# A PV pass between query projection and scores, and a new order of five key and value loads, in an attention and gated-FFN kernel

## The chip, the cores and the metric

The kernel runs on one core of one Trainium2 chip. The metric is device time in microseconds of one execution. A profile belongs to one execution, and its span is 1.8 to 2.1 us shorter than the time on the clock.

The engines are PE (TensorE, matmul), PEld (its weight loads, which overlap with matmuls), DVE (VectorE), ACT (ScalarE), POOL (GpSimd) and SP (which issues most transfers). "Head m" counts the 64 pairs of a block of 512 queries and one of 16 heads: four blocks, 16 heads each. "k6" and "v5" are the keys and values of the seventh and sixth of eight key/value heads; heads 10 and 11 read k5 and v5, heads 12 and 13 read k6 and v6.

## The reference, cut to what matters

```python
xn = layernorm(x)                                   # [1, 2048, 448]
q  = (xn @ wq) as 16 heads of 256
k, v = the last 512 rows of k_cache, v_cache, each of 8 heads used by 2 query heads
s  = softmax(q k^T / 16) v, heads joined, @ wo      # scores: 2048 x 512 a head
g  = silu((gelu(xn @ w_gate) * (xn @ w_up)) @ w_down)
return x + s * g
```

## The kernel before

Everything is recorded as operations with the buffers that they read and write; a small planner gives each a place on its engine and puts in the semaphore waits. FFN first, then attention. In attention PE alternates between a *query group* (the projection of 4, 6 or 8 heads by matmuls of 64 rows, two of which run side by side) and a run of scores and PV, 128 rows each.

```python
def q_group(n, pairs, more_act=False):        # two heads, four PSUM banks
    ...
    group(units, 0, QC, True, True)           # 64-row matmuls
    for i, b in enumerate(pairs):             # PSUM -> qT, half on ACT, half on DVE
        act(qT[:, s, 0, :], bank[b], ACT.Copy, (b_ps[b],), (b_qT[s][0],))
        ...
def s_mm(m):                                  # scores of one head: 4 tiles of 128 queries
    for t4 in range(4):
        b = AB[t4]
        mms([... qT x kT, 2 matmuls ...], [b_kT[g]] + b_qT[s], (b_ps[b],))
        ... ACT: p = exp(bank), row sums;  every second tile, DVE: 1/sum, pn = p * 1/sum
        dma_t(pT[...], pn[...])               # every second tile: transposed by a transfer

def pv(m):                                    # 8 matmuls: 2 halves e of 4 key blocks j
    for e in range(2):
        b = BB[m % 2 * 2 + e]
        mms([... va x pT ... for j in range(NJ)], [b_va[g]] + b_pT[x], (b_ps[b],))
        ... oTh <- bank on ACT or DVE
...
for m in range(NS):                           # NS = 64, LAG = 2
    if m in groups:                           # 0, 4, 12, 18, 26, 34, 42, 50, 58
        for i in range(m, hi, 2):
            p = (i - m) // 2
            q_group(i, ((cur, nxt[::-1], (cur[1], nxt[1])) if three else (cur, nxt) * 2)[p], end)
            ...
            if m == Q0 + QS and p == 0:       # m = 12
                K.reuse(...)
                for g in range(6, Hkv):
                    load_k(g)                 # transposing transfer
                for g in range(5, Hkv):
                    load_v(g)                 # plain transfer
                ...                           # Pool: 2 loads of g, 3 of x
    s_mm(m)
    ...
    if len(late) == LAG:
        pv(late.pop(0))                       # PV of head m-2
    ...
    late.append(m)
```

So PE's order in a run is: scores of m, PV of m-2, scores of m+1, PV of m-1, and so on. A PV has from its scores to its start two heads' time for exp, normalizing and the transposing transfer.

The softmax here doesn't subtract the row's maximum and nothing guards it: scores larger than these inputs give would overflow.

Of the kernel before, what the change touches and what calls it, by code (L numbers as in the profile page):

```python
# [168 lines left out]
def bass_recurrent_scan__sliding_block_cached__geglu_ffn__prompt_kernel(  # L169
# [13 lines left out]
    Hkv, Sk, Dh = A_k_cache.shape[1], A_k_cache.shape[2], A_k_cache.shape[3]  # L183
    HD = A_wq.shape[1]
    Hq = HD // Dh
# [6 lines left out]
    NJ = W // P  # L192
# [12 lines left out]
    Q0 = 4  # L205
# [6 lines left out]
    with es:  # L212
# [14 lines left out]
        def sbuf_bufs(at, size, n):  # L227
            return [K.buf(at + i * size, size) for i in range(n)]
# [35 lines left out]
        b_va = sbuf_bufs(a, NJ * Dh * 2, Hkv)  # L264
# [75 lines left out]
        b_pT = [sbuf_bufs(a + i * QC * NJ * 2, QC * NJ, 2) for i in range(NPT)]  # L340
# [25 lines left out]
        b_ps = [K.buf() for i in range(8)]  # L366
# [4 lines left out]
        groups = [0, Q0, Q0 + QS, Hq + 2] + list(range(Hq + 2 + QS, NQC * Hq, QS)) + [NQC * Hq]  # L371
# [181 lines left out]
        def bk(pairs, j):  # L553
            return pairs[j // 2] + j % 2
# [156 lines left out]
        def load_v(g):  # L711
            dma("sp", va[:, g, :, :],
                A_v_cache[0, g, Sk - W:Sk, :].rearrange("(j p) d -> p j d", p=P), (), (b_va[g],))
# [36 lines left out]
        cur, nxt = (0, 2), (4, 6)  # L750
        for n in range(4, NU, 2):
# [6 lines left out]
            cur, nxt = nxt, cur  # L758
# [24 lines left out]
            if n + 1 in DOWN_AT:  # L783
                def norms():
                    for f in (ln_a, ln_a, ln_b, ln_b):
                        f()
                end = down7(DOWN_AT[n + 1], (cur[0], cur[0] + 1, cur[1], cur[1] + 1, nxt[0], nxt[0] + 1),
                            (g2x[:, 0:2, :], g2x[:, 2:4, :]), b_g2x, then=norms if n < 28 else None)
                end(0, 1)
                end(2, 3)  # L790
                cur, nxt = (nxt[1], cur[1]), (cur[0], nxt[0])
# [10 lines left out]
        def q_group(n, pairs, more_act=False):  # L802

            c, h = divmod(n, Hq)
            units = [(b, lambda j, k, i=i: wq[:, k, (h + i) * Dh + j * P:(h + i) * Dh + (j + 1) * P],
                      wqr[:, h + i, :], slice(c * QC, (c + 1) * QC), b_wql[h // HG][:1], b_wql[h // HG][1:], b_xnT[c * 4:c * 4 + 4])
                     for i, b in enumerate(pairs)]
            group(units, 0, QC, True, True)
            for i, b in enumerate(pairs):
                s = qs(n + i)  # L810
                act(qT[:, s, 0, :], bank[b], ACT.Copy, (b_ps[b],), (b_qT[s][0],))
                if more_act and i:
                    act(qT[:, s, 1, :], bank[b + 1], ACT.Copy, (b_ps[b + 1],), (b_qT[s][1],))
                    continue
                K.op("dve", lambda v, s=s, b=b: v.tensor_copy(qT[:, s, 1, :], bank[b + 1]),  # L815
                     (b_ps[b + 1],), (b_qT[s][1],))

        AB, BB = [], []
        LAG = 2
        NS = NQC * Hq  # L820

        def s_mm(m):
            s, g = qs(m), m % Hq // 2
            for t4 in range(4):
                b = AB[t4]
                mms([(bank[b], qT[:, s, e, t4 * P:(t4 + 1) * P], kT[:, g, e, :], e == 0, e == 1) for e in range(2)],
                    [b_kT[g]] + b_qT[s], (b_ps[b],))
                n = m * 4 + t4
                r, z, y, x = n % NRS, n % NP32, n // 2 % NPN, n // 4 % NPT
                K.op("act", lambda e, b=b, r=r, z=z: e.activation(  # L830
                    p32[:, z, :], bank[b], ACT.Exp, scale=att_scale, accum_out=rsum[:, r:r + 1]),
                    (b_ps[b],), (b_p32[z], b_rsum[r]))
                if t4 % 2 == 1:
                    K.op("dve", lambda e, r=r: e.reciprocal(rden[:, r - 1:r + 1], rsum[:, r - 1:r + 1]),  # L834
                         b_rsum[r - 1:r + 1], b_rden[r - 1:r + 1])
                    for t in range(2):
                        K.op("dve", lambda e, r=r - 1 + t, z=(n - 1 + t) % NP32, y=y, t=t: e.tensor_scalar(  # L837
                            pn[:, y, t, :], p32[:, z, :], rden[:, r:r + 1], None, op0=ALU.mult),
                            (b_p32[(n - 1 + t) % NP32], b_rden[r - 1 + t]), (b_pn[y],))
                    dma_t(pT[:, x, t4 // 2, :, :, :].rearrange("p t j q -> p (t j) q"),  # L840
                          pn[:, y, :, :].rearrange("p t k -> p (t k)"), (b_pn[y],), (b_pT[x][t4 // 2],))

        def pv(m):
            h = m % Hq
            g, x = h // 2, m % NPT
            for e in range(2):
                b = BB[m % 2 * 2 + e]
                mms([(bank[b].rearrange("p (t q) -> p t q", q=P), va[:, g, j, e * P:(e + 1) * P],
                      pT[:, x, :, :, j, :].rearrange("p a t q -> p (a t) q"), j == 0, j == NJ - 1)
                     for j in range(NJ)], [b_va[g]] + b_pT[x], (b_ps[b],))  # L850
                i = 2 * h + e
                if e == 0 or m >= NS - LAG:
                    act(oTh[:, i, :], bank[b], ACT.Copy, (b_ps[b],), (b_oT[i],), scale=WS)
                else:
                    K.op("dve", lambda v, i=i, b=b: v.tensor_scalar(  # L855
                        oTh[:, i, :], bank[b], WS, None, op0=ALU.mult), (b_ps[b],), (b_oT[i],))
# [131 lines left out]
        late = []  # L988
# [6 lines left out]
        AB.extend(bk(cur, j) for j in range(4))  # L995
        BB.extend(bk(nxt, j) for j in range(4))
        for m in range(NS):
            if m in groups:
                hi = groups[groups.index(m) + 1]
                three = hi - m == 6  # L1000
                for i in range(m, hi, 2):
                    end = m > Hq and m % Hq == LAG
                    p = (i - m) // 2
                    q_group(i, ((cur, nxt[::-1], (cur[1], nxt[1])) if three else (cur, nxt) * 2)[p], end)
                    if m == 0:
                        sum_act(2, 2 + p)
                    if m == Q0 and p == 0:
                        K.reuse(b_kT[2:6] + b_va[3:5])
                        for g in range(2, 6):
                            load_k(g)  # L1010
                        for g in range(3, 5):
                            load_v(g)
                    if m == Q0 and p < 2:
                        gates3(2 * p)
                        gates3(2 * p + 1)
                    if m == Q0 + QS and p == 0:
                        K.reuse(b_kT[6:] + b_va[5:] + [b for y in b_xr for b in y])
                        for g in range(6, Hkv):
                            load_k(g)
                        for g in range(5, Hkv):  # L1020
                            load_v(g)
                        now = [[o for o in K.ops if o.eng == "pe"][-1]]
                        for t in range(NG2):
                            load_g2(t, now)
                        for t in range(NXR):
                            dma("pool", xr[:, t, :], x_view[:, t, :], (), b_xr[t], now)
                    if end and p:
                        burst_end((m // Hq - 1) * 4 + p - 1)
                    if m > Hq and m % Hq == LAG + QS and p == 1:
                        burst_end((m // Hq - 1) * 4 + 3)  # L1030
                if m == 0:
                    K.reuse([b for x in b_pT for b in x] + b_pn + b_p32)
            if m > Hq and m % Hq == LAG:
                K.reuse(b_pn + b_p32)
            s_mm(m)
            if m < LAG:
                if m == 0:
                    gates2 = down7(2, (BB[0], BB[1], AB[2], AB[3], BB[2], BB[3]), g2w, b_g2w, (3, 4, 6, 5, 2, 1),
                                   lambda: [sum_act(3, k) for k in range(4)])
                else:  # L1040
                    gates3 = down7(3, (BB[1], BB[0], AB[2], AB[3], BB[2], BB[3]), g2w, b_g2w, (3, 4, 2, 5, 6, 1),
                                   lambda: [gates2(q) for q in range(4)])
                    K.reuse(b_pT[2])
                if m == LAG - 1:
                    K.reuse(b_oT + [b for y in b_qT[:QS - Q0] for b in y])
                    assert not CASTS and not SUMS
            if len(late) == LAG:
                pv(late.pop(0))
            if m > Hq and m % Hq == LAG - 1:
                if m // Hq == 1:  # L1050
                    for b in [y for x in b_xs for y in x]:
                        b.old.extend(y for t in range(4) for z in b_xnT[t] for y in z.readers + [z.writer])
                burst(m // Hq - 1)
            late.append(m)
# [56 lines left out]
```

## Time and profile before

| | before |
|---|---|
| time, median of the first 3 runs | 540.66 us (540.63 to 542.68) |
| span of the profiled execution (a seventh run, 541.98 us on the clock) | 540.2 us |
| PE busy | 533.2 us, 99% |
| ACT, DVE busy | 58%, 71% |
| transfers of the instruction stream | 33 packets, 0.54 MB |
| pT transposes | 128, median 2.8 us from issue to landing |

The last two rows come from these lines of the page (queue and kind: packets, MB, share of 16 engines; and a transfer: count, median us to landing):

```profile
q8 instruction: 33, 0.54, 0.4%
...
pT<-pn SPq DMA_TRANSPOSE x128, 2.8
```

A note for reading PE: the profile gives each 512-column matmul a duration of 379 ns, while they follow each other every 216 ns. A gap of less than about 0.16 us is therefore no idle time in the profile. All gaps below are worked out from starts: start of the first matmul after the gap, minus start of the last before, minus 0.216. When a matmul's record is missing, its weight load, which is always recorded, stands for it.

### The profile page before, as it was taken

The numbers are of one execution on the slowest core, as the hardware profiler recorded it, in microseconds if no ns is written. First come the engines' busy times: TensorE is split into PE (matmuls) and PEld (weight loads), VectorE is DVE, ScalarE is ACT, GpSimd is POOL, SyncE is SP. The second block draws the span as 40 slices with busy tenths as digits, with TensorE's granted clock in tenths as the row PEclk, the third lists the DMA queues.
The fourth block names the chain that finished last, engine by engine and source line by source line (L and its number), as shares of the span: only waits on it lengthen the run. The fifth ranks groups of instructions, "written<-read, shape, count | busy, mean of one in ns | idle before, by whom it ended". The sixth has DMA issues, their size and how long they took to land.

```text
span 540.2 us, 10920 instructions
## 1 busy us (share of the span) xinstructions
PE 533.2 (99%) x4155; PEld 310.6 (58%) x4180; DVE 383.6 (71%) x839; ACT 314.2 (58%) x782; POOL 39.7 (7%) x78
## 2 busy tenths in 40 slices
PE   9999999999999999999999999999999999999998
PEld 5556656459644444984444469544444884444487
DVE  6689886798767757934875786367667934776785
ACT  5466355873568768116866850488488106876820
POOL 1131120000000010003001000120000003001010
PEclk9999999999999999999999999999999999999999
DMA  9569173932598686302861860067448302872821
GB/s 296 123 187 108 53 126 87 282 70 60 112 171 138 156 190 147 59 1 82 167 141 50 152 137 1 18 156 139 96 106 146 72 1 69 164 157 73 149 66 35
DMA packets 171604, 61.38 MB, mean 114 GB/s; under 512 B 155104, under 2 KB 168416, under 8 KB 171552
## 3 DMA queue, kind: packets, MB, share of 16 engines
q1 hardware_dynamic: 167488, 51.30, 45.0%
q0 software_dynamic: 3008, 8.72, 6.9%
q8 instruction: 33, 0.54, 0.4%
q10 hardware_dynamic: 1056, 0.66, 0.4%
q14 instruction: 19, 0.16, 0.1%
HBM read 19.76 MB, written 3.67 MB: 43 GB/s over the span
## 4 chain that ended last, share of the span: by engine, by line
PE 87%; ACT 4%; DMA 4%; DVE 3%; issue 1%; SPq 1%; ACTq 0%; DVEq 0%
PE bank L394 86%; ACT p L830 4%; DMA pT<-pn 2%; DVE pn L837 2%; DMA va<-in_A_v_cache_dram 1%; PE bank L511 1%; DVE rden L834 1%; SPq L382 1%; PE bank L492 0%; DVE oTh L855 0%; ACT oTh L385 0%; DVE xnT L884 0%; DVE gl L424 0%; DVE xnT L388 0%; DVE epst L425 0%
## 5 line engine op out<-in xcount | busy, mean ns | idle before, releaser
L830 ACT ACTIVATE p<-bank 128x512 f32<-128x512 f32 x256 | 150.6, 596 | 28.9 <-DVE pn L837 26.5
L394 PE MATMUL bank<-pT,va 128*128 128x512 bf16 x512 | 120.9, 379 | 0.8 <-DMA pT<-pn 0.5
L394 PE MATMUL bank<-kT,qT 128*128 128x512 bf16 x487 | 117.8, 379 | 2.3 <-ACT qT L385 1.0
L837 DVE TENSOR_SCALAR pn<-p,rden 128x512 bf16<-128x512 f32 x256 | 112.9, 483 | 8.7 <-DMA pT<-pn 4.4
L394 PE MATMUL bank<-xnT,wq 64*128 64x512 bf16 x768 | 94.9, 376 | 0.0
L394 PEld LDWEIGHTS bank<-pT,va 128*128 128x128 bf16 x512 | 49.4, 98 | 62.5 <-DMA pT<-pn 3.2
L394 PEld LDWEIGHTS bank<-kT,qT 128*128 128x128 bf16 x512 | 49.3, 98 | 61.7 <-issue 3.4
L394 PE MATMUL bank<-xnT,wgu 64*128 64x512 bf16 (+2 forms) x768 | 83.9, 350 | 0.1
L385 ACT ACTIVATE qT<-bank 128x512 bf16<-128x512 f32 x76 | 44.1, 596 | 51.6 <-PE bank L394 50.0
L815 DVE CAST qT<-bank 128x512 bf16<-128x512 f32 x52 | 34.8, 690 | 49.4 <-PE bank L394 49.4
L394 PEld LDWEIGHTS bank<-xnT,wq 64*128 64x128 bf16 x768 | 36.7, 94 | 46.3 <-ACT p L830 1.7
L394 PEld LDWEIGHTS bank<-xnT,wgu 64*128 64x128 bf16 x768 | 37.6, 94 | 36.0 <-issue 0.5
L834 DVE RECIPROCAL rden<-rsum 128x2 f32<-128x2 f32 x128 | 21.1, 165 | 48.3 <-ACT p L830 48.2
L830 ACT ACTIVATION_READ_ACCUMULATOR p<-bank 128x1 f32 x256 | 51.6, 202 | 0.0
L394 PE MATMUL bank<-wt,sr 128*128 128x224 f16 x512 | 50.0, 259 | 0.0
L394 PEld LDWEIGHTS bank<-wt,sr 128*128 128x128 f16 x512 | 49.0, 98 | 0.4 <-ACT oTh L385 0.2
L385 ACT ACTIVATE gl<-bank 128x512 bf16<-128x512 f32 x56 | 33.0, 596 | 26.4 <-PE bank L394 22.1
L560 DVE TENSOR_TENSOR actTh<-bank,gl 128x512 f16<-128x512 f32 x56 | 37.4, 688 | 11.3 <-PE bank L394 5.8
L855 DVE TENSOR_SCALAR oTh<-bank 128x512 f16<-128x512 f32 x62 | 42.3, 683 | 0.0
L385 ACT ACTIVATE oTh<-bank 128x512 f16<-128x512 f32 x66 | 38.9, 590 | 3.8 <-PE bank L394 3.8
L394 PE MATMUL bank<-wt,oTh 128*128 128x224 f16 (+1 forms) x416 | 38.4, 252 | 0.0
L394 PEld LDWEIGHTS bank<-wt,oTh 128*128 128x128 f16 x416 | 37.2, 98 | 0.9
(77 smaller groups left out, 387.8 us busy)
## 6 DMA issues: line engine op xcount, KB each, us to landing
wtb<-in_A_wo_dram POOLq DMA_DIRECT2D x4, 896.0 KB, 10.8
wq<-in_A_wq_dram SPq DMA_DIRECT2D x2, 1536.0 KB, 7.9
va<-in_A_v_cache_dram SPq DMA_DIRECT2D x8, 256.0 KB, 6.3
pT<-pn SPq DMA_TRANSPOSE x128, 2.8
xr<-in_A_x_dram POOLq DMA_DIRECT2D x15, 112.0 KB, 2.3
wd<-in_B_w_down_dram SPq DMA_DIRECT2D x1, 1568.0 KB, 7.5
g<-g_all POOLq DMA_DIRECT2D x14, 112.0 KB, 2.3
out_dram<-xr POOLq DMA_DIRECT2D x12, 112.0 KB, 2.1
```

What stands on the lines that cost most here:

```text
L382: K.op("sp", lambda e, o=o, i=i: e.dma_start_transpose(o, i), reads, writes, dma=True)
L385: K.op("act", lambda e, o=o, i=i: e.activation(o, i, func, scale=scale), reads, writes)
L394: ins = e.matmul(o, lhsT=l, rhs=r, start=st, stop=sp, skip_group_check=True)
L511: ins = e.matmul(bank[b][:, 0:w], lhsT=gl[:, 0, 0:P], rhs=gl[:, 0, 0:w], start=True, stop=True)
L560: K.op("dve", lambda e: e.tensor_tensor(actTh[:, c % 2, f, :], bank[b + 1], gl[:, s, :], ALU.mult), (b_ps[b + 1], b_gl[s]), (b_actT[c % 2] ...
L815: K.op("dve", lambda v, s=s, b=b: v.tensor_copy(qT[:, s, 1, :], bank[b + 1]), (b_ps[b + 1],), (b_qT[s][1],))
L830: K.op("act", lambda e, b=b, r=r, z=z: e.activation(p32[:, z, :], bank[b], ACT.Exp, scale=att_scale, accum_out=rsum[:, r:r + 1]), (b_ps[b] ...
L834: K.op("dve", lambda e, r=r: e.reciprocal(rden[:, r - 1:r + 1], rsum[:, r - 1:r + 1]), b_rsum[r - 1:r + 1], b_rden[r - 1:r + 1])
L837: K.op("dve", lambda e, r=r - 1 + t, z=(n - 1 + t) % NP32, y=y, t=t: e.tensor_scalar(pn[:, y, t, :], p32[:, z, :], rden[:, r:r + 1], None, ...
L855: K.op("dve", lambda v, i=i, b=b: v.tensor_scalar(oTh[:, i, :], bank[b], WS, None, op0=ALU.mult), (b_ps[b],), (b_oT[i],))
```

## The change

It aims at two kinds of waits. At six of the nine places where a query group ends and scores begin (heads 4, 18, 26, 34, 42 and 50), PE's list of waits names the copy of q out of PSUM; at the other three (0, 12 and 58) it shows a wait of the same kind with no cause, as "issue". At heads 12, 26, 34, 42, 50 and 58 one PV matmul, ready long before, now goes between. And at head 12 PV of head 10 waits for v5, which was issued behind k6 and k7; now v5 goes first. The banks of the last two query pairs are placed anew so that the PV matmul's bank is free early.

```diff
-        def pv(m):
+        def pv(m, part=None):
...
-                     for j in range(NJ)], [b_va[g]] + b_pT[x], (b_ps[b],))
+                     for j in range(NJ) if part is None or (part == 0) == (e == j == 0)], [b_va[g]] + b_pT[x], (b_ps[b],))
+                if part == 0:
+                    break
...
+            split = m in groups and m not in (0, Q0, Hq + LAG)
...
-   q_group(i, ((cur, nxt[::-1], (cur[1], nxt[1])) if three else (cur, nxt) * 2)[p], end)
+   q_group(i, ((cur, nxt[::-1], (cur[1], nxt[1])) if three else (cur, nxt, (cur[0], nxt[0]), (cur[1], nxt[1])) if split else (cur, nxt) * 2)[p], end)
...
+                        load_v(5)
                         for g in range(6, Hkv):
                             load_k(g)
-                        for g in range(5, Hkv):
                             load_v(g)
...
+            if split:
+                pv(late[0], 0)
             s_mm(m)
...
-                pv(late.pop(0))
+                pv(late.pop(0), 1 if split else None)
```

## The prediction

> **What bounds the kernel now.** I read the page's busy shares first, then the list of waits of PE, then the timeline of PE around the places that the change touches, then the chain of waits, and last the record of every transfer from issue to landing.
>
> The busy shares, the two largest matmul groups of the score stage (columns: busy us, mean ns of one, idle before) and PE's own list of waits:
>
> ```profile
> PE 533.2 (99%) x4155; PEld 310.6 (58%) x4180; DVE 383.6 (71%) x839; ACT 314.2 (58%) x782; POOL 39.7 (7%) x78
> ...
> L394 PE MATMUL bank<-pT,va 128*128 128x512 bf16 x512 | 120.9, 379 | 0.8 <-DMA pT<-pn 0.5
> L394 PE MATMUL bank<-kT,qT 128*128 128x512 bf16 x487 | 117.8, 379 | 2.3 <-ACT qT L385 1.0
> ```
>
> ```profile
> PE bank L394 <- ACT qT L385: 1.0, 6, 0.2
> ...
> PE bank L394 <- DMA pT<-pn: 0.5, 2, 0.3
> PE bank L394 <- DMA va<-in_A_v_cache_dram: 0.2, 1, 0.2
> ```
>
> PE is the bound from the first microsecond to the last: 533.2 of 540.2 us, at full granted clock. All that PE waits for by name is some 3 us. Two of these rows are what the change aims at: six waits of 0.2 us for the copy of q out of PSUM, at the six places where a query group gives way to scores, and one wait for v. So the whole prize, taken at face value, is 1.0 + 0.2 = 1.2 us of 540, or 0.2%.
>
> A busy share hides gaps, though, because a matmul's record lasts 379 ns while eight of them follow each other in 1.73 us, which is 0.216 us apart. So I worked from start times. The timeline of PE at head 26, the third of the six places, and the weight loads there, then the weight loads at the first down projection (49.9 us), where no query group is near:
>
> ```profile
> 289.72 1.46 PE L394 MATMUL bank<-xnT,wq 64*128 64x512 bf16 x12
> 291.33 1.67 PE L394 MATMUL bank<-kT,qT 128*128 128x512 bf16 x7 [0.16 <-ACT qT L385]
> 292.85 1.89 PE L394 MATMUL bank<-pT,va 128*128 128x512 bf16 x8
> ...
> 291.11 1.41 PEld L394 LDWEIGHTS bank<-kT,qT 128*128 128x128 bf16 x8 [0.42 <-issue]
> ```
>
> ```profile
> 49.91 0.50 PEld L394 LDWEIGHTS bank<-wdh,actTh 128*128 128x128 f16 x6 [0.42 <-issue]
> ```
>
> Two things are to be seen. Only seven of the eight score matmuls have a record, but all eight weight loads do, from 291.11 on: the first score matmul ran at about 291.12 and its record is missing. The "0.16 us wait" is mostly that hole. Second, the weight load before it came 0.305 us after the last 64-row matmul (290.800 to 291.105), and so did the one at 49.9 us (49.605 to 49.909), which goes from 64-row to 128-row matmuls as well and has nothing to do with q. The copy that the list names ended at 291.17, after the weight load had already begun, so it cannot have held it. The same distance (0.53 us with the hole) stands at all of the query-group ends, whatever ACT was doing. The real loss is the step from 64-row to 128-row tiles: 0.305 + 0.015 - 0.2 (normal distance of a pair to the next) = about 0.12 us each.
>
> The place where PE does wait is head 12, the third query group (chain of waits in that stretch, columns: start, us, what):
>
> ```profile
> 189.43 1.30 SPq L382
> 190.73 0.05 issue
> 190.78 1.29 SPq L382
> 192.07 0.04 issue
> 192.12 6.26 DMA va<-in_A_v_cache_dram
> 198.38 0.05 issue
> 198.42 1.68 PE bank L394 x7
> ```
>
> The two SPq entries are the issues of k6 and k7, 1.3 us each; v5 is issued only behind them, lands at 198.38, and PV of head 10 starts at 198.42. The last score matmul began at 197.86, and PV would have followed at 198.07. PE lost **0.35 us** there.
>
> **What the Trainium skill says.** "TensorEngine Tiling (Array Packing)", Key Properties: changing the tiling mode drains TensorE, changing the tile does not. The trace agrees, 0.12 us per change in either direction (0.10 from PV back to the query projection). "Perfetto Trace Analysis", Tensor Engine Instruction: the end of a matmul in a profile is computed, not observed. It agrees: 379 ns for what repeats every 216 ns, hence starts and not ends above. "DMA: Bandwidth & Descriptors", Queues, rings and completion order: transfers of one issuing engine are consumed in ring order, while different queues share the same 16 engines by turns. It agrees: k6, with nothing of Pool's beside it, took 3.19 us from issue to landing; k7, beside the g and xr loads that Pool issues from 190.66 on, took 5.34, and v5 behind it 6.26.
>
> **The change part by part.**
>
> *PV pass ahead of the scores (six places).* It moves one matmul of 0.216 us from behind the eight score matmuls to before them. The order listing shows the same 4180 matmuls and one semaphore instruction less on PE. PE's work is unchanged. The change from 64 to 128 rows stays, as PV has 128 rows too; only who pays it changes. Removed: about 0. The new waits: PV of head m-2 needs pT of that head (landed 9 to 35 us earlier), v, and its PSUM bank. To have this bank free, the last two query pairs are placed anew: its copy now stems from the third pair, which ended 3 us earlier. In exchange the third and fourth score tiles take banks that the fourth pair filled. At head 26 these copies end at 291.17 (ACT) and 291.26 (DVE), the third tile would need its bank at about 292.2: 0.9 us to spare. At heads 34, 50 the final sums of the burst stand before the copies on DVE, but the copy still ends at 352.65, when the tile needs it at 353.8. So no new wait here.
>
> *Scores 0.216 us later.* The exps of the first head start 0.65 us after its first weight load and would start 0.22 us later. Its transposed pT then lands 0.22 us later, for a PV that comes at the same time as before. I compared the landing of both halves of pT with the PV that reads them, head by head: first heads 12, 26, 42 and 58 have 1.58, 1.18, 1.19 and 1.18 us of slack. Heads 34 and 50 have 0.04, but there the first exp is held by an extra copy on ACT (it starts 1.09 us after, not 0.65), so it does not move. From the second head on, exps start when their tile is ready and the delay is made up. Cost: 0, at worst a few hundredths.
>
> *v5 first at head 12.* v5 would be issued at 189.43 in place of 192.12. When v3 followed a row of k loads at 156 us, it landed 1.8 us after the last of them; the transfer before v5 now lands at 190.88, so I estimate 192.7 for v5. It is needed earlier than before, at 196.34, since its PV pass now opens the scores. That leaves 3.6 us: the wait goes, **-0.35 us**. k6 is now second. It is needed at 196.34 + 0.22 = 196.56. In the kernel before, k7 in that position (beside Pool's five loads) landed 3.5 us after k6 (192.63 to 196.11). An estimate for k6: 192.7 + 3.5 = 196.2, 0.3 us before its need. v6, k7 and v7 are read from 203 us on and are safe.
>
> Sum: -0.35 (v5), 0 from the six passes, +0.1 as the mean of k6 being a little late: about -0.25 to -0.35, 540.66 - 0.3 = **540.4 us**.
>
> **Rivals.**
>
> *The waits for q are real.* Then six passes of 0.216 us each cover six waits of 0.16, together 1.0, and with v5 the time is 539.3. For it: the list of waits. Against: the missing record, the weight load that started before the named copy ended, and the same 0.42 us at 49.9 us.
>
> *k6 takes the place of v5.* With copies and transposes in turn and Pool's loads between, k6 could take as long as v5 did, 6.3 us from about 190.05, so 196.35, or as the slowest k (8.4 us), 198.4. The late case stops PE for up to 1.9 us with the PV pass already spent, and the time is 541 to 542. For it: every transfer from 190.7 to 193.3 took 4.6 to 7.5 us. Against: k6 stands second in its ring and most of that queue was behind it.
>
> *Shifted DMA coincidences.* Some pT transposes land 1 to 2 us late and stop PE (0.48 us at 174.97, 0.28 at 378.77, 0.34 at 419.05). In the packet records a 16 KB instruction packet precedes each of these by 3 to 4 us. They depend on phase; shifting the stream by 0.2 to 0.35 us can make one of them some tenths better or worse. This is worth plus or minus 0.3 us and has no preferred sign.
>
> **Range and chances.** The three runs before span 540.63 to 542.68, and two agree within 0.03. Gain fully kept: 540.3. Rival one would give 539.3, rival two 541 to 542; I give them one chance in ten and one in six. The 8-in-10 range is 539.6 to 541.2. 2% is 10.8 us, nine times all the PE waiting that the change could touch, so faster 0.005, within 2% 0.985, slower 0.01 (should k6 or v5 lag far beyond any transfer seen).
>
> **What would show it right or wrong.** Right: the PE wait for v is gone, v5 lands before 196.3 and k6 before 196.5, and at each of the six places the distance from the last 64-row matmul to the first 128-row weight load is still 0.30 us, now with a PV weight load. Wrong: that distance falls to about 0.2 us or below (the waits for q were real); PE's list shows a wait for k at head 12 (rival two); or the span changes by more than half a microsecond with the gap at head 12 accounting for less than that, with late pT transposes in other places (rival three).

## The result, and the profile after

| | before | changed |
|---|---|---|
| median of 6 runs each | 541.25 us (540.63 to 542.68) | 540.68 us (540.47 to 541.23) |
| ratio | | 0.9989, 95% interval 0.9975 to 1.0003 |
| span of the profiled execution | 540.2 us | 538.7 us |

A ratio is the mean time of one kernel's fast runs over that of the other's of the same rounds, so it isn't quite the ratio of the medians. The interval contains 1: no difference is shown. The time is within the predicted range and 0.28 us above the predicted value. The two profiled spans, however, differ by 1.46 us, five times the gain that was predicted, and that had to be explained. On the clock these two executions took 541.98 and 540.47 us: one 0.73 us above the median of its kernel, the other at the lowest of its kernel's times.

PE's waits in the changed kernel, the whole list (what was waited for: us in total, times, longest):

```profile
PE bank L511 <- DVE epst L425: 1.2, 1, 1.2
PE bank L492 <- DVE xn L467: 0.5, 1, 0.5
PE bank L394 <- ACT qT L385: 0.3, 2, 0.2
PE bank L394 <- issue: 0.2, 1, 0.2
```

The wait for v is gone, that for pT too, and of the six waits for the copy of q two are left, at heads 4 and 18, where the change puts nothing. Taken at its word, the list says that the change did all it was meant to. Head 26, matmuls first and then weight loads:

```profile
288.78 1.46 PE L394 MATMUL bank<-xnT,wq 64*128 64x512 bf16 x12
290.17 0.39 PE L394 MATMUL bank<-pT,va 128*128 128x512 bf16 x1
290.62 1.67 PE L394 MATMUL bank<-kT,qT 128*128 128x512 bf16 x7
```

```profile
290.17 0.10 PEld L394 LDWEIGHTS bank<-pT,va 128*128 128x128 bf16 x1 [0.42 <-issue]
290.18 1.61 PEld L394 LDWEIGHTS bank<-kT,qT 128*128 128x128 bf16 x8
```

No idle time is named before the PV matmul, but the weight load still stands 0.42 us idle as before, and it comes 304 ns after the last 64-row matmul, as before. At all six places this distance is 304 or 305 ns in both kernels. The hole of a missing score record is still there too, at 290.40: only now a PV record stands ahead of it. From the last 64-row matmul to the first 128-row matmul are 308 or 309 ns after. Before, that record is missing; runs 1 and 3 below, the order of PE at these places unchanged and no record missing, show 308 or 309 as well. The second 128-row matmul comes 534 or 535 ns after the last 64-row one before; after, its record is the missing one, and in the second profile of the changed kernel (run 2) it comes at 534 or 535 too. So the six PV passes saved nothing, to within 2 ns each.

Head 12, the issues of the transfers and then the chain of waits of the same stretch:

```profile
188.87 0.57 SPq L379 DMA_DIRECT2D va<-in_A_v_cache_dram  x1
189.50 1.23 SPq L382 DMA_TRANSPOSE kT<-in_A_k_cache_dram  x1
```

```profile
186.98 9.17 PE bank L394 x83
196.15 0.05 issue
196.20 3.83 PE bank L394 x17
```

v5 is issued first and landed at 192.00, k6 at 194.84; they were needed at 195.76 and 195.98. The chain, which before ran through two SP issues and a transfer of 6.26 us, is PE and 0.05 us of issue.

The 1.46 us between the spans add up from starts: the first scores began 0.08 us earlier (noise of the start), 0.36 us of waiting for v are gone, and the gaps behind late pT are 1.27 us in the profile before (0.49, 0.07, 0.29, 0.34 and two under 0.06) and 0.30 us in the profile after, 0.97 less: together 1.41. The last 0.05 us fits the restart after a gap: the second matmul behind it follows after 226 or 227 ns in place of 216, at seven gaps before and at one after. Two thirds of the difference are thus in a thing that the change does not touch.

### The profile page after: what moved, and what is told of

Its sections match the earlier page's. It is cut to its first block, busy times and chain, and to the rows that moved or that the text cites. A ratio compares the mean times of both kernels' runs of the same rounds, so it can differ in the third digit from the quotient of the medians.

```text
span 538.7 us, 10915 instructions
## 1 busy us (share of the span) xinstructions
PE 532.6 (99%) x4155; PEld 311.0 (58%) x4180; DVE 383.7 (71%) x839; ACT 314.4 (58%) x782; POOL 39.6 (7%) x78
## 4 chain that ended last, share of the span: by engine, by line
PE 97%; DMA 1%; DVE 1%; ACT 0%; issue 0%
PE bank L394 97%; DMA pT<-pn 1%; DMA x<-in_A_x_dram 0%; ACT p L830 0%; DVE stats L441 0%; PE bank L492 0%; DVE pn L837 0%; ACT oTh L385 0%; DVE xn L467 0%; DVE mv L444 0%; PE bank L511 0%; DVE xnT L887 0%; DVE xnT L388 0%; DVE rden L834 0%; DVE rstd L461 0%
```

## The experiments

"Theory" in what follows is the prediction's: the query waits are the step between tile modes, v5 is the only gain, the rest is chance. Rival one takes the waits in the list as real; another takes the late-pT gaps as fixed by the program. Runs 1 to 4 shared one chip and its runs of the kernel before, as did 5 to 8, 9 to 11, and 12.

### 1 and 2: both kernels once more

No edit.

> A second profile of the kernel before, and a control of the timing. Theory (changed kernel gains 0.35 us by the earlier v5, 0.06 by the six passes, and the rest of the 1.5 us between the two profiled spans is late pT transposes that fall differently from one execution to the next): the PE gap before PV of head 10 is again 0.3 to 0.4 us and the six distances from the last 64-row matmul to the first 128-row weight load again 0.305 us, but the PE gaps behind late pT (0.48, 0.28 and 0.34 us in the first profile) are of other sizes or in other places, and their sum (1.1 us) differs by some tenths; the ratio in time is 1.000 within 0.002. Rival (those gaps are fixed by the order of the program, so the change removed them): the same gaps at the same places within 0.05 us.

> A second profile of the changed kernel. Theory: no gap at head 10's PV, the six distances 0.305 us again, late-pT gaps different from the first profile of it (which had one of 0.30 us at 377 us); ratio to before 0.9985 to 0.9995. Rival: the late-pT gaps are the same as in its first profile, 0.8 us less than in the kernel before, and the ratio is 0.997 to 0.998.

Before again: 541.53 us, ratio 1.0003 (0.9991 to 1.0015). Changed again: 541.82 us, ratio 1.0010 (0.9994 to 1.0026), so this time on the other side of 1, and outside the 0.9985 to 0.9995 that was expected. The second profile of the kernel *before*, first the whole list of PE's waits, then its score and PV matmuls at head 26:

```profile
PE bank L394 <- DMA pT<-pn: 1.6, 2, 1.5
PE bank L511 <- DVE epst L425: 1.2, 1, 1.2
```

```profile
291.97 1.90 PE L394 MATMUL bank<-kT,qT 128*128 128x512 bf16 x8
293.71 1.46 PE L394 MATMUL bank<-pT,va 128*128 128x512 bf16 x6
```

The same place in the second profile of the *changed* kernel, where no record is missing either:

```profile
290.62 0.39 PE L394 MATMUL bank<-pT,va 128*128 128x512 bf16 x1
290.85 1.89 PE L394 MATMUL bank<-kT,qT 128*128 128x512 bf16 x8
292.57 1.67 PE L394 MATMUL bank<-pT,va 128*128 128x512 bf16 x7
```

From the first 128-row matmul to the PV after the scores are 1.74 us without the pass and 1.95 us with it: one matmul of 0.21 us more ahead, and one less behind.

The kernel before has no wait for the copy of q at all in this profile. All eight score records of head 26 happen to be there, and the idle time with them is gone. The weight load comes 304 ns after the last 64-row matmul, as always. The named wait was a missing record and nothing else. (Of the fourteen profiles, seven lack 25 score records: before, changed, runs 5 to 8 and 12. The other seven lack none.)

The gaps behind late pT fell elsewhere. The largest of any undisturbed profile is in this one:

```profile
260.78 1.89 PE L394 MATMUL bank<-kT,qT 128*128 128x512 bf16 x8
264.13 1.90 PE L394 MATMUL bank<-pT,va 128*128 128x512 bf16 x8 [1.46 <-DMA pT<-pn]
```

Eight score matmuls from 260.78 take 1.73 us, so PV was due at 262.51: a gap of 1.62 us. In sum these gaps are 1.27 and 2.12 us in the two profiles of the kernel before, 0.30 and 1.14 in those of the changed one. The spread between two executions of one program (0.85 us) is as large as the difference between the kernels, so the first pair of profiles owed two thirds of its difference to chance. The wait for v before PV of head 10 was 0.36 us in the first profile and 0.07 in the second, which misses the 0.3 to 0.4 that I expected.

### 3: the order of loads alone

```diff
+                        load_v(5)
                         for g in range(6, Hkv):
                             load_k(g)
-                        for g in range(5, Hkv):
                             load_v(g)
```

> The kernel before with the new order of loads alone (v5, then k6, v6, k7, v7), no PV pass ahead. Theory: v5 lands at about 192, six us before its PV needs it; k6 lands at about 195, a little over one us before the first scores need it at 196.3; the gap of 0.35 us before PV of head 10 is gone; that is all of the gain, about -0.35 us, ratio 0.9993. The named waits for the copy of q (six of 0.16 us) stand as before. Rival (waits for q are real and the six passes take them away): this part gives a third of the gain of the whole change or less.

541.66 us, ratio 1.0006 (0.9994 to 1.0018). v5 landed at 192.34 and k6 at 195.27, 0.8 us before the first scores of head 12 loaded their weights (196.07), and the gap at PV of head 10 is nil. The six named waits did not "stand as before": they are not in this profile's list, though nothing that could remove them was changed. In time the gain is not resolved.

### 4: five PV passes alone

```diff
+            split = m in groups and m not in (0, Q0, Q0 + QS, Hq + LAG)
```
with the old order of loads and the rest of the change.

> The kernel before with the PV pass ahead of the scores at five places (heads 26, 34, 42, 50, 58, not 12) and the old order of loads. Theory: the named waits for q at these five disappear from the list, because the first record after the step is then a PV record that is not missing, but the distance from the last 64-row matmul to the first 128-row weight load stays 0.30 us; gain 5 x 0.01 = 0.05 us, ratio 1.000 within noise; the gap at head 10 stays 0.35 us. Rival (waits for q real): the distance shrinks to 0.2 us or below at the five, gain 5 x 0.16 = 0.8 us, ratio 0.9985.

541.50 us, ratio 1.0005 (0.9994 to 1.0017). The distance from the last 64-row matmul to the first 128-row weight load is 304 or 305 ns at all eight places from head 4 on, with and without the pass. (That the named waits are gone from the list says nothing here: this profile lacks no record.) Rival one, which wanted 200 ns or less and 0.8 us, falls by the trace; the time agrees but could not have told 0.8 us safely. The gap at head 10 did *not* stay at 0.35: v5 landed at 197.20 and PV, due at 197.44, did not wait.

### 5: the PV pass at head 12 without the new order

```diff
+                        for g in range(6, Hkv):
+                            load_k(g)
+                        for g in range(5, Hkv):
+                            load_v(g)
```
in the changed kernel, in place of its own loads.

> The changed kernel with the old order of loads (k6, k7, v5, v6, v7), so the PV pass of head 10 stands before the scores of head 12 and v5 still comes last but two. Theory: v5 lands at about 198.4 and the pass, wanted at 196.34, holds the scores behind it until then: a gap of 2.0 us in place of 0.35, so about 1.6 us slower than the kernel before, ratio 1.003; so the new order is what the PV pass at head 12 can't do without. Rival (the pass covers a wait of its own length): slower by 1.4 us at most, or not at all.

542.18 us, ratio 1.0013 (0.9991 to 1.0034). PE around head 12:

```profile
195.02 1.46 PE L394 MATMUL bank<-xnT,wq 64*128 64x512 bf16 x12
197.80 0.38 PE L394 MATMUL bank<-pT,va 128*128 128x512 bf16 x1 [1.33 <-issue]
```

v5 landed at 197.71 and the pass stood until then: its weight load came 1.67 us after the last 64-row matmul in place of 0.30, so 1.37 us were lost where 2.0 was expected. The mechanism is as said and the size smaller, again because v5 came earlier than in the first profile. The two parts of the change belong together: the pass asks for v5 1.73 us sooner, and only the new order provides it.

### 6: all of PV ahead of the scores

```diff
-                pv(late[0], 0)
+                pv(late.pop(0))
             s_mm(m)
...
-                pv(late.pop(0), 1 if split else None)
+                pv(late.pop(0))
```

> The changed kernel with all eight PV matmuls (1.73 us) ahead of the scores at the six places, in place of one. Tests the slack that the prediction read: pT of the first head lands 1.16 to 1.58 us before its PV, or 0.04 at heads 34 and 50. Theory: scores 1.73 us later, then two heads' scores back to back; PE stops behind the exps or the transposes by about 0.5 us at heads 12, 26, 42 and 58 and about 1.2 us at 34 and 50: 3 to 5 us slower than the changed kernel, ratio to before 1.005 to 1.008. Rival (more PV ahead hides more of the wait for q): not slower than the changed kernel.

544.54 us, ratio 1.0049 (1.0027 to 1.0071), the first difference that the time shows. Weight loads from head 26 on:

```profile
292.45 2.47 PEld L394 LDWEIGHTS bank<-kT,qT 128*128 128x128 bf16 x12
295.19 0.16 PEld L394 LDWEIGHTS bank<-kT,qT 128*128 128x128 bf16 x2 [0.27 <-ACT p L830]
296.06 0.11 PEld L394 LDWEIGHTS bank<-kT,qT 128*128 128x128 bf16 x2 [0.70 <-ACT p L830]
```

Two heads' scores stand back to back, and the last tiles of the second wait for the exps of the first. That is 0.37 us of PE at each of the six places, 2.2 us in all. More PV ahead hides nothing, since there was nothing to hide. My expectation for heads 34 and 50, 1.2 us, was wrong: they wait 0.37 us for the exps like the others, and behind that only 0.11 and 0.01 us for pT.

### 7 and 8: what the step between tile modes costs

26 small matmuls between groups of 64-row matmuls in the FFN, far from any query copy, with 128 rows or with 64:

```diff
         for n in range(4, NU, 2):
+            mms([(bank[cur[0]][:, 0:64], ident[0:128, :], ident[0:128, 0:64], True, True)], (b_ident,), b_ps[cur[0]:cur[0] + 2])
             gu_group((n, n + 1), cur)
```
(and `ident[0:64, ...]` twice for the control). The group's own first matmul overwrites the result, so the output stays right.

> The kernel before with one small matmul of 128 rows and 64 columns ahead of each of 26 gate and up groups of 64-row matmuls, overwritten by the group's own first matmul. Measures what the step between 64 and 128 rows costs where no copy of q is near. Theory: each costs 0.11 us into 128 rows, 0.10 us back and about 0.03 us itself, 0.24 us; 26 times, less two that stand behind a 128-row product: about 5.9 us slower, ratio 1.011. Rival (the step is free, the 0.12 us at the query groups is a wait): about 0.8 us slower, as with 64 rows.

> The control of the run before: the same 26 small matmuls with 64 rows in place of 128, so that no step between tile modes is added. Theory: about 0.03 us each, 0.8 us in all, ratio 1.0015. Rival: as slow as with 128 rows.

With 128 rows 547.64 us, ratio 1.0108 (1.0090 to 1.0126), so +5.8 us for 5.9 expected. With 64 rows 542.63 us, ratio 1.0017 (1.0002 to 1.0032), so +0.9 us for 0.8 expected. The weight loads of the score matmuls, with 128 and then with 64 rows (durations, then first and last start):

```profile
L394 PEld LDWEIGHTS bank<-kT,qT x512: 95/98/99, 123.5 to 516.3; 128*128 128x128 bf16 x171
```

```profile
L394 PEld LDWEIGHTS bank<-kT,qT x512: 95/98/99, 118.2 to 511.2; 128*128 128x128 bf16 x171
```

The scores begin at 123.5 and 118.2 us (117.5 in the kernel before), a difference of 5.3 us that no late pT has touched yet. Two of the 26 stand behind a 128-row product and add no step; at 23 of the other 24 the small matmul of 128 rows starts 308 or 309 ns after the last 64-row one, as the first 128-row matmul does at the query groups. In time, 5.3 / 24 = 0.22 us for the step there and back, as the 0.12 + 0.10 us read from the trace before. The distance at the query groups is thus the price of the step, measured where no copy of q is near.

### 9 and 12: why pT is late

In nine profiles (before, changed, and runs 1 to 5, 7 and 8), I compared each pT transpose with the packets in flight beside it, from 1 us ahead of its issue to its landing. With neither an instruction packet nor a Pool transfer there, none of 666 took over 3.5 us, median 2.73. With an instruction packet (and no Pool transfer), 187 of 351 did. So I put plain transfers of 16 KB beside the transposes, at 60 heads. First as a copy of two rows, which the trace shows as 16 packets of 1 KB each:

```diff
+            if m >= Q0:
+                dma("pool", scr[m], A_wq[m:m + 2, :], (), (b_scr[m],), [[o for o in K.ops if o.eng == "dve"][-1]])
             if len(late) == LAG:
                 pv(late.pop(0))
```

> The kernel before with one plain copy of 16 KB (DRAM to an unused DRAM tensor, from Pool's queue) at each of 60 heads, released by the same DVE result as the second pT transpose of the head. Tests why pT lands late: over nine profiles, none of 666 transposes with neither an instruction packet nor a Pool transfer in flight took over 3.5 us from issue to landing (median 2.73), and 187 of 351 with an instruction packet of 16 or 8 KB did. Theory (a plain transfer, however small, holds up transposes in flight): the transposes beside the copies take 4 us or more, past their slack of 1.16 us, PE stops 0.3 to 0.5 us at most of the some 48 heads whose PV follows without a query group between, 12 to 25 us slower, ratio 1.02 to 1.045. Rival (coincidence, or a matter of bytes: 16 KB is 0.14 us at the mean 114 GB/s): the slack swallows it, ratio within 1.001.

542.49 us, ratio 1.0019 (1.0006 to 1.0033), for 1.02 to 1.045 expected. The theory as it stood fell: of 76 transposes that had a Pool transfer beside them (nearly always such a copy) and no instruction packet, two took over 3.5 us. The 1 us lost is more than the rival allowed, and what it goes to is open. But those copies were packets of 1 KB of 0.05 us each, while the instruction packet is a single one of 16 KB that takes 1.1 us (median of 33), or of 8 KB (0.3 to 1.5 us; these are counted too). "DMA: Bandwidth & Descriptors" of the Trainium skill, section on why a DMA increments its semaphore by 16, says that a transfer is dealt out over the largest number of engines, up to 16, that divides the slowest dimension that isn't of size 1, on both sides. A row of 8,191 elements (a prime) can't be divided, and the trace of the run below agrees, with one packet for each copy:

```diff
-                dma("pool", scr[m], A_wq[m:m + 2, :], ...
+                dma("pool", scr[m], wq_flat[m:m + 1, 0:8191], ...
```

> As e9, which refuted that any plain transfer holds up transposes (of 76 transposes with only a small copy in flight two took over 3.5 us). There the 16 KB went as 1 KB packets[...], 0.05 us each; an instruction packet is one packet of 16 KB, which takes 1.1 us (median)[...]. Here each of the 60 copies is one row of 16,382 bytes, so one packet on one engine. Theory (one long packet on one of the engines is what makes pT late): transposes beside the copies take 3.2 to 4.5 us in place of 2.73, some of them past the slack of 1.16 us; PE stops 0.1 to 0.4 us at a good part of some 48 heads, 4 to 15 us slower, ratio 1.007 to 1.03. Rival (it is the instruction fetch itself that matters, for example a stop of the queue that issues the transposes): as e9, ratio 1.000 to 1.003.

552.64 us, ratio 1.0200 (1.0183 to 1.0217). The trace has 60 packets of 16,382 bytes, median 0.97 us. Transfers of run 9 and then of run 12 (KB each, median us from issue to landing), and then PE's weight loads by what they waited for in run 12:

```profile
pT<-pn SPq DMA_TRANSPOSE x128, 2.8
scratch<-in_A_wq_dram POOLq DMA_DIRECT2D x60, 16.0 KB, 2.1
```

```profile
pT<-pn SPq DMA_TRANSPOSE x128, 3.8
scratch<-in_A_wq_dram POOLq DMA_DIRECT2D x60, 16.0 KB, 3.1
```

```profile
PEld bank L394 <- DMA pT<-pn: 18.1, 29, 1.6
```

The same number of bytes, at the same places, in one packet each: the median transpose goes from 2.8 to 3.8 us, 81 of the 120 from head 4 on take over 3.5 us (22 in run 9), and 10.8 us are lost. The profiled execution was the slowest of the five, 555.33 us; in it 9.6 us are gaps behind late pT and 3.3 us a late v5 at head 12. A single long packet beside a transpose delays it; the same bytes in short packets don't. The runs differ in the number of packets too, and the trace does not say which DMA engine a packet took. So the length of the packet is not told apart from all bytes passing through a single engine; many short packets on one engine were not tried. That an instruction packet acts in the same way is the likely reading of its 1.1 us and of the counts above. It is not shown directly, since no run here could move or shorten one.

### 10 and 11: more time for pT

If late pT costs PE 0.3 to 2.1 us an execution, more room between scores and PV should recover it. The first score tile of the next head goes ahead of each PV too:

```diff
-            s_mm(m)
+            s_mm(m, range(1 if ahead else 0, 4))
+            ahead = LAG <= m < NS - 1 and m + 1 not in groups
+            if ahead:
+                s_mm(m + 1, (0,))
```
(in the changed kernel; run 11 adds the copies of run 9.)

> The changed kernel, with the first score tile (two matmuls, 0.43 us) of the next head also ahead of each PV inside a query group, so that PV reads pT 0.43 us later after its scores. Theory: the slack of pT grows from 1.16 to some 1.6 us, the late-pT gaps of PE (0.3 to 2.5 us in sum in the profiles so far) shrink to under 0.4 us in sum, apart from the largest; ratio to before 0.997 to 0.999. Rival (exps are then the bound, as the exp of the next head stands before the copy of PV's result on ACT): new waits of PE for the exps, ratio 1.000 or above.

> The 60 small copies of e9 in the kernel of e10. If lateness of pT past its slack is what costs in e9, then 0.43 us more slack takes 0.3 to 0.43 us off each of the some 48 stops: this kernel is 10 to 20 us faster than e9. Rival (the copies cost otherwise): as slow as e9.

Run 10: 540.76 us, ratio 0.9996 (0.9981 to 1.0011). PE's list of waits in it has one row left:

```profile
PE bank L511 <- DVE epst L425: 1.2, 1, 1.2
```

No gap behind late pT remains in that execution, and 0.09 us of a wait of a score tile came in. Its span is 538.9 us, though, no better than the 538.7 of the changed kernel's lucky first profile (its scores began 0.46 us later, at 117.87; from there on it is 0.21 us shorter), and the time shows no gain. Run 11: 541.98 us, ratio 1.0008 (0.9990 to 1.0026). As run 9 had lost only 1 us, the 10 to 20 us that I expected to recover were not there, and the run tells nothing about the slack. One of its last PVs waited 1.99 us for pT, so 0.43 us more room does not cover every case. Neither kernel beats the two in question by anything that can be measured.

## Why the prediction was right or wrong

**The bound** was read rightly: PE is busy for 532.6 of 538.7 us after.

**The waits for q** were rightly set at nothing. The distance of 304 ns did not move in the changed kernel or in run 4, the named wait vanished by itself in runs 1 and 3, and runs 7 and 8 measured the step at 0.22 us there and back where 0.22 had been read (the 0.12 of it is 0.11 with the 0.213 us that the trace shows from one pair to the next, rounded there to 0.2). The sum had 0 for the six passes, and with all records there (runs 1 and 2) it is 0; the 0.06 us that my expectation for run 1 gave them has no such support. Two readings on the way were wrong, without effect on the sum. The six waits named for q are not at the six places of the change: two are at heads 4 and 18, and those at 12 and 58 are named "issue". And the 0.04 us called slack at heads 34 and 50 is none: there PV waits for pT (gaps of 0.07 and 0.03 us in the profile before) and starts 0.04 us after the landing.

**Scores 0.22 us later** cost nothing, as said. First heads 26, 42 and 58 have 0.97, 0.96 and 0.97 us of slack after in place of 1.18, 1.19 and 1.18, and the second heads are back at 1.16. At 34 and 50 the first exp starts 1.09 us after the first 128-row weight load in both kernels, so it did not move.

**v5 first** was right in its mechanism and wrong in its size, and this is the step that failed in the sum: the whole gain forecast rests on it. The prediction took 0.35 us from the one profile that it had. Six profiles now have the old order and no pass at head 12 (before, runs 1, 4, 7, 8, 9; run 12 with its long packets is left out): 0.36, 0.07 and four times 0. The mean is 0.07 us. v5 lands within some tenths of its need, sometimes before and sometimes after; the profile before was the worst of the six. The landing itself, estimated at 192.7, was at 192.0 to 192.7 in the four profiles with the new order and the kernel otherwise near this one (changed twice, run 3, run 10).

**k6 in second place** was in time: 194.84, for an estimate of 196.2 and a need of 195.98 (that profile runs 0.57 us ahead of the first at this place). The 0.1 us set aside for it was not needed.

**Shifted coincidences** were rightly named as having no sign, and undersized. The prediction gave them 0.3 us; two executions of one program differ by 0.84 to 0.85 us in this alone. That is two thirds of the 1.46 us between the spans.

Put together, the gain that the traces support is the 0.07 us of v5, or 0.01%, where 0.3 was predicted. The two timings, 0.9989 and 1.0010, can't tell either from zero. The predicted time was met because the range was wide enough for the noise; that the median came within 0.28 us of it is luck, as the gain it was worked out from is mostly not there.

## What to carry to other kernels

A wait named in a profile deserves a second profile of the same program before it is believed or attacked: here six of the waits were missing records, and a seventh was the worst of six draws. Take starts, not ends and names, for an engine that is 99% busy, and measure a disputed cost by multiplying it where nothing else is near, as runs 7 and 8 did. If transposing transfers are on the path, watch whether what runs beside them goes as long packets, and not only how many bytes it is.

## What the Trainium skill lacked or had wrong

- "TensorEngine Tiling (Array Packing)", Key Properties, has that a change of mode drains TensorE and gives no cost. Here it is some 0.1 us from two 64-row tiles to 128 rows and as much back (runs 7 and 8: 0.22 us for both).
- "Runtime: NRT & Kernel Launch", Instruction fetch mechanics, calls the cost of crossing a 16 KiB boundary "mostly hidden". The cost on the issuing side isn't visible here, but 187 of 351 transposes that had an instruction packet and no Pool transfer beside them took over 3.5 us, against 0 of 666 with neither, and PE gaps of up to 1.62 us followed such transposes.
- "DMA: Bandwidth & Descriptors", Queues, rings and completion order, says that an engine turns to another queue only after a whole packet. That a long packet can hold up a transpose fits this, but the page has no cost for it. 60 packets of 16 KB cost 10.8 us, the same bytes in 1 KB packets about 1 us.
- "Perfetto Trace Analysis" says that the end of a matmul is computed, which is right, but not that records can be missing and turn up as a wait for another engine. Here 25 of 512 score matmuls have no record in seven of fourteen profiles, and six waits of 0.16 us for the copy of q in the first rest on that.
